# A new tile order for the first convolution of a two-layer attention and long-convolution kernel, with later spectrum stores and earlier exchanges

## The chip, the core and the metric

The kernel runs on one core of a Trainium2 chip. The metric is the device time in microseconds (us), the median of several runs. A profile of one execution gives, beside it, every instruction of the engines: PE (TensorE, matrix products), ACT (ScalarE), DVE (VectorE), POOL (GpSimd) and the DMA queue that SyncE issues (SP). The engines run side by side, each through its own list of instructions in program order, and wait for each other by semaphores. So the *order* in which the program lists its tiles decides which engine waits for which.

## The reference, cut to what matters

Two layers of the same pair are applied to x (2048 positions, 512 channels): a sliding dilated attention `A`, and a long convolution `B` through a Fourier transform.

```python
def _B_ref(u, A_re, A_im, B_re, B_im, C_re, C_im, log_dt, Dskip):
    ...                                            # K: the filter, 512 channels x 2048 taps
    Kp = jnp.pad(K, ((0, 0), (0, L)))
    up = jnp.pad(up, ((0, 0), (0, 0), (0, L)))     # up is u, transposed to channels x positions
    Kf = rfft2(Kp[:, None, :]); Uf = rfft2(up[:, :, None, :])      # abbreviated
    Yf = Uf * Kf[None, :, :, :]
    y = irfft2(Yf, s=(1, L2))[:, :, 0, :L]
    return y.transpose(0, 2, 1) + u * Dskip[None, None, :]

x = x + _A_ref(_layernorm(x), A_wqkv, A_wo)
x = x + _B_ref(_layernorm(x), ...)     # "first convolution": computes Uf and Kf
x = x + _A_ref(_layernorm(x), A_wqkv, A_wo)   # "second front": its layernorm, transposes, K and Q projections
x = x + _B_ref(_layernorm(x), ...)     # the same filter: Kf is read back from memory
```

## The kernel before

The part that matters is the first convolution and what follows it up to the first product of the second attention. The transforms are products on PE in two steps. Work is cut into tiles of 128 x 1024 elements, and each tile goes PE -> two PSUM banks -> a copy ("evacuation") to SBUF by ACT or DVE. A string of tokens fixes the order, and the last letter of a token says who evacuates: `A` is ACT, `D` is DVE.

```python
ORDER0 = """
KA KD KA KD KA KA KD KA KD KA KD kA KD KA KA kD kA kD kA UA KD UA UA UD UA kD UA
UA UD KA UA kD u kD m u u u kA m UA m UD UA u kA m kD u UA u m UA m
UD m UA kA u kD kD u kA u m m kA m u u yD yA m u u m u m yA u yA
yA m m yA m yA yD
"""
ORDERF = """
yA yA yA yA yA yA z00D yA h00 yA z01D h01 z10A z11A h10 a0 p0 h11
n0 z12A z02A a1 z03A h12 S T0 h02 p1 E00A n1 E01A a2 z13A P00 h13 Q00
h03 T1 E10A p2 E11D P01 a3 P02 P03 P10 p3 P11 n2 n3 P12 T2 E20D E21A
P13 T3 E30A P20 P21 x1 P22 P23 E31D
"""
```

There are 16 tokens each of `K` (first step of the filter's transform), `U` (the same of the signal), `k` and `u` (second step), `m` (product of the spectra, on DVE) and `y` (first step back): eight for each of two groups of channels. `z` is the last step (PE, then an addition into x on DVE, or a copy by ACT when PE has added x too). In the second string, `h`, `a`, `p` and `n` are the layernorm's statistics, their sum, its reciprocal root (ACT) and its application (DVE). `T` and `E` are the transposes and their evacuation, `P` and `Q` the projections (four matmuls of 512 columns and one ACT copy), `x` a shifted copy on DVE.

```python
def ptile(self, shape):                     # PSUM tiles: two pools of two, so four in flight
    self.npt += 1
    return self.ps[(self.npt - 1) // 2 % len(self.ps)].tile(shape, F32, name="pb", tag="pb")

def evac(self, dst, src, eng):              # L726
    (self.nc.scalar.copy if eng == "act" else self.nc.vector.tensor_copy)(dst, src)

def k_f2(self, g, ec, eng):
    n = g * NEC + ec
    p2 = self.f2(g, "ka", ec)               # 16 matmuls of 64 columns, L744
    kf = self.nat[n] = self.free.pop(0)     # a slot of SBUF
    self.evac(kf, p2, eng)
    self.nk += 1
    self.pump()
    self.nc.sync.dma_start(self.kf_dram[g, ec]..., kf...)      # L754: store for the second layer

def open_ring(self):                        # called after the last K: eight more slots
    kp2 = self.ring_pool.tile([P, 8, DQG, EC], BF16, name="kf_nat", tag="kp")
    self.free += [kp2[:, i] for i in range(8)]

def pump(self):
    while self.nkf < min(self.nk, self.nm + self.ahead):       # ahead = 4
        self.kf_load(self.nkf); self.nkf += 1

def kf_load(self, n):                       # "exchange": odd and even partitions change places
    kn, ks = self.nat[n], self.free.pop(0)
    for h in range(2):
        sync.dma_start(ks[h::2], kn[1 - h::2])                  # L770
    self.kf[n] = kn, ks

def u_mult(self, g, ec):                    # m: needs ub (from u), kn and its exchanged copy ks
    kn, ks = self.kf.pop(n); ub = self.ub.pop(n)
    for t, k in zip(self.S[g]["t"], (kn, ks)):
        self.nc.vector.tensor_tensor(t[...], ub[:], k, ALU.mult)   # L784
    self.nm += 1
    if self.tag == 0:
        self.free += [kn, ks]
    self.pump()

def u_f2(self, g, ec):                      # u: ub has three buffers; evacuated by ACT, L796
    ...

def i1(self, g, t, eng):                    # y: 16 matmuls of 128 columns, L809/L810
    ...
```

Twelve slots are there from the start. The end of the first attention's layernorm is run beside the first `K` tokens, one closure after each `K` from the second on:

```python
return [lambda: [u_end(8), u_apply(8, range(8, 12), "pool")], lambda: x_stats(14), lambda: x_stats(15),
        lambda: u_begin(12, 16, "dve", "act"), lambda: [u_end(12), u_apply(12, range(12, 16), "pool")]]
```

`u_begin(12, 16, "dve", "act")` sums the statistics on DVE and takes the reciprocal root on ACT, both under one token.

Of the kernel before, what the change touches and what calls it, by code (L numbers as in the profile page):

```python
# [14 lines left out]
F32 = mybir.dt.float32  # L15
# [5 lines left out]
P = 128  # L21
S = 2048
# [15 lines left out]
NG = 2  # L38
DQG = 64
EC = 16  # L40
NEC = 128 // EC
# [6 lines left out]
WUTUxlkKkUkEKkzUzKpzUUqkEzUxpUKxtUUUUUetpqxekQUkkpxKUUkKkpUxEXkkxpUXKXxqpXXqXQgkpKZZZgxx  # L48
"""
ORDER0 = """  # L50
KA KD KA KD KA KA KD KA KD KA KD kA KD KA KA kD kA kD kA UA KD UA UA UD UA kD UA
UA UD KA UA kD u kD m u u u kA m UA m UD UA u kA m kD u UA u m UA m
UD m UA kA u kD kD u kA u m m kA m u u yD yA m u u m u m yA u yA
yA m m yA m yA yD
"""
ORDERF = """
yA yA yA yA yA yA z00D yA h00 yA z01D h01 z10A z11A h10 a0 p0 h11
n0 z12A z02A a1 z03A h12 S T0 h02 p1 E00A n1 E01A a2 z13A P00 h13 Q00
h03 T1 E10A p2 E11D P01 a3 P02 P03 P10 p3 P11 n2 n3 P12 T2 E20D E21A
P13 T3 E30A P20 P21 x1 P22 P23 E31D  # L60
"""
ORDER1 = """
UD UA UA UD UA UA UD UA UD UA UD u UD u m UA u u m UA m u u UA m UD m
# [35 lines left out]
def row_stats(nc, lnst, x_row, a, eng):  # L99
    if eng == "dve":  # L100
        nc.vector.bn_stats(lnst["bn"][:, a, 0, :], x_row)
    else:
        nc.scalar.activation(lnst["junk"][:], x_row, ACT.Identity, accum_out=lnst["s1"][:, a:a + 1])
        row_sumsq(nc, lnst, x_row, a)
# [11 lines left out]
def rstd_act(nc, pool, var):  # L116
    rstd = pool.tile(list(var.shape), F32, name="ln_rstd")
    nc.scalar.activation(rstd[:], var, ACT.Ln, bias=EPS)
    nc.scalar.activation(rstd[:], rstd[:], ACT.Exp, scale=-0.5)
    return rstd  # L120


def ln_begin(nc, pool, lnst, a0, a1, eng, rs="pool"):
    n = a1 - a0
    if eng == "dve":
        ag = pool.tile([P, n, 2], F32, name="ln_ag")
        for a in range(n):
            nc.vector.bn_aggr(ag[:, a, :], lnst["bn"][:, a0 + a, 0, :])
        var, mean, ms = ag[:, :, 1], ag[:, :, 0], -1.0
    else:  # L130
        mean, ms = lnst["s1"][:, a0:a1], -1.0 / D
        msq = pool.tile([P, n], F32, name="ln_msq")
        nc.vector.scalar_tensor_tensor(msq[:], mean, -1.0 / (D * D), mean, ALU.mult, ALU.mult)
        veps = pool.tile([P, n], F32, name="ln_veps")
        nc.vector.scalar_tensor_tensor(veps[:], lnst["s2"][:, a0:a1], 1.0 / D, msq[:], ALU.mult, ALU.add)
        var = veps[:]
    if rs == "act":
        return rstd_act(nc, pool, var), mean, ms
    rstd = pool.tile([P, n], F32, name="ln_rstd")
    nc.vector.tensor_scalar(rstd[:], var, EPS, None, ALU.add)  # L140
    nc.gpsimd.tensor_tensor(rstd[:], rstd[:], lnst["mh"][:, 0:n], ALU.pow)
    return rstd, mean, ms


def ln_end(nc, pool, st):
    rstd, mean, ms = st
    nb = pool.tile(list(rstd.shape), F32, name="ln_nb")
    nc.vector.scalar_tensor_tensor(nb[:], mean, ms, rstd[:], ALU.mult, ALU.mult)
    return rstd, nb
# [6 lines left out]
def ln_apply(nc, out_ap, in_ap, rstd, nb, a, eng):  # L156
    if eng == "act":
        nc.scalar.activation(out_ap, in_ap, ACT.Identity, bias=nb[:, a:a + 1], scale=rstd[:, a:a + 1])  # L158
    else:
        (nc.gpsimd if eng == "pool" else nc.vector).tensor_scalar(out_ap, in_ap, rstd[:, a:a + 1], nb[:, a:a + 1], ALU.mult, ALU.add)  # L160


class LayerA:
# [143 lines left out]
    def core(self, x_sb, u, lnp, ev=None, nprod=0):  # L307

        tc, nc, lnst, l = self.tc, self.nc, self.lnst, self.layer
# [12 lines left out]
        with ExitStack() as c2:  # L322
# [69 lines left out]
            pvs, oTs, lns = {}, {}, {}  # L392
# [20 lines left out]
            def out_proj(a):  # L413
                oT = oTs.pop(a)
                pw = pq_tile()
                xr = x_sb[:, a, :]
                nc.tensor.matmul(pw[:], lhsT=ident[:], rhs=xr, start=True, stop=False)
                for ftp in range(NDT):
                    nc.tensor.matmul(pw[:], lhsT=oT[:, ftp, :], rhs=wo[:, ftp, :], start=False, stop=(ftp == NDT - 1))  # L419
                if a >= 12:  # L420
                    if a >= 14 and l == 1:
                        row_stats(nc, lnst, pw[:], a, "dve")
                    nc.scalar.copy(xr, pw[:])
                else:
                    nc.scalar.activation(xr, pw[:], ACT.Identity, accum_out=lnst["s1"][:, a:a + 1])
                    row_sumsq(nc, lnst, xr, a)

            def x_stats(a):
                row_stats(nc, lnst, x_sb[:, a, :], a, "dve")

            def u_begin(a0, a1, eng, rs="pool"):
                lns[a0] = ln_begin(nc, lnp, lnst, a0, a1, eng, rs)

            def u_end(a0):
                lns[a0] = ln_end(nc, lnp, lns[a0])

            def u_apply(a0, rows, eng=None):
                rstd, nb = lns[a0]
                for a in rows:
                    ln_apply(nc, u[:, :, a, :], x_sb[:, a, :].rearrange("p (q r) -> p q r", r=4), rstd, nb, a - a0,  # L440
                             eng or ("dve" if a % 2 else "act"))
# [47 lines left out]
            for n in range(16):  # L489
# [11 lines left out]
                if n in (8, 12):  # L501
                    u_end(n - 8)
# [12 lines left out]
                if n == 15:  # L515
                    x_stats(13)
                    if l == 1:
                        u_end(8)
                        u_apply(8, range(8, 12), "dve")
# [4 lines left out]
                event(("o", n))  # L524
            if l == 0:
                out_proj(15)
                return [lambda: [u_end(8), u_apply(8, range(8, 12), "pool")], lambda: x_stats(14), lambda: x_stats(15),
                        lambda: u_begin(12, 16, "dve", "act"), lambda: [u_end(12), u_apply(12, range(12, 16), "pool")]]
            u_begin(12, 15, "dve", "act")
            out_proj(15)  # L530
            pw = pq_tile()
# [155 lines left out]
class FftB:  # L687
# [59 lines left out]
    def k_f2(self, g, ec, eng):  # L747
        n = g * NEC + ec
        p2 = self.f2(g, "ka", ec)
        kf = self.nat[n] = self.free.pop(0)  # L750
        self.evac(kf, p2, eng)
        self.nk += 1
        self.pump()
        self.nc.sync.dma_start(self.kf_dram[g, ec].rearrange("p r q e -> (p r) (q e)"), kf.rearrange("p q e -> p (q e)"))  # L754

    def open_ring(self):
        kp2 = self.ring_pool.tile([P, 8, DQG, EC], BF16, name="kf_nat", tag="kp")
        self.free += [kp2[:, i] for i in range(8)]

    def pump(self):  # L760
        while self.nkf < min(self.nk, self.nm + self.ahead):
            self.kf_load(self.nkf)
            self.nkf += 1

# [14 lines left out]
    def u_mult(self, g, ec):  # L779
        n = g * NEC + ec  # L780
        kn, ks = self.kf.pop(n)
        ub = self.ub.pop(n)
        for t, k in zip(self.S[g]["t"], (kn, ks)):
            self.nc.vector.tensor_tensor(t[:, :, ec * EC:(ec + 1) * EC], ub[:], k, ALU.mult)  # L784
        self.nm += 1
        if self.tag == 0:
            self.free += [kn, ks]
        self.pump()

# [457 lines left out]
def kernel(  # L1247
# [16 lines left out]
    nc = tc.nc  # L1264
# [6 lines left out]
    with tc.tile_pool(name="ctmp", bufs=1) as tmp:  # L1271
        consts = build_a_consts(tc, nc, cpool, tmp)
    lnst = dict(s1=cpool.tile([P, NA], F32, name="ln_s1"), s2=cpool.tile([P, NA], F32, name="ln_s2"),
                bn=cpool.tile([P, NA, 2, 6], F32, name="ln_bn"), junk=cpool.tile([P, D], BF16, name="ln_junk"),
                mh=cpool.tile([P, 4], F32, name="ln_mh"))
# [7 lines left out]
    u = xnT[:].rearrange("p t (b r) -> p (t b) r", r=64).rearrange("p q (a r) -> p q a r", r=4)  # L1283
# [5 lines left out]
    lnp = ctx.enter_context(tc.tile_pool(name="ln_small", bufs=3, reuse_waits="tile"))  # L1289
# [5 lines left out]
    kp = kpp.tile([P, P, NA, 4], BF16, name="k_perm", tag="kp")  # L1295
# [26 lines left out]
    with tc.tile_pool(name="ctmp_g2", bufs=1) as g2tmp, tc.manual_schedule(engines=MAN):  # L1322
# [9 lines left out]
        late = la.core(x_sb, u, lnp, ev, 3)  # L1332
# [4 lines left out]
    fb = FftB(tc, nc, C, consts["ident"], w2_dram, g2_dram, kf_dram, x_sb, 0)  # L1337
# [1 line left out]
    fb.ahead = 4  # L1339
    fb.open_mid()  # L1340
    with tc.manual_schedule(engines=MAN):
        fb.run(ORDER0, u, k=kp, late=late)
    fb.c_mid.close()
    la.close()
    la = LayerA(tc, nc, consts, lnst, A_wqkv, A_wo, 1, xnT, 1)
# [1 line left out]
    with tc.manual_schedule(engines=MAN):  # L1347
# [21 lines left out]
        def last(*ops):  # L1369
            def f():  # L1370
                for op, *ix in ops:
# [6 lines left out]
                     e=lambda ft: la.front_ext(3, "dve", ft))  # L1378
        fb.run(ORDERF, None, more=front)
        la.front_close()  # L1380
# [11 lines left out]
    fb = FftB(tc, nc, C, consts["ident"], w2_dram, g2_dram, kf_dram, x_sb, 1)  # L1392
# [48 lines left out]
```

## Time and profile before

| | before |
|---|---|
| device time, median of three runs | 435.77 us (435.69 to 436.33) |
| span of the profiled execution | 434.5 us |
| busy over the span: PE, DVE, ACT | 351.9, 393.2, 322.4 us |
| first matmul of the first convolution | 202.32 us |
| last product `m` of the first convolution | 252.46 us, 0.69 us long |
| first product of the second attention (L295) | 287.98 us |

Times are counted from the start of the span. A row of the groups or of the timeline names the line, the engine, the operation, the tile written, the tiles read, the shapes and the number of instructions. Behind it stand the time and, in brackets, the idle time before it and what ended it. The chain of waits is the path followed back from an end to its causes, and "windows" give each engine's busy time in a stretch. A busy time sums durations that overlap a little, so the step from one instruction's start to the next on the same engine is the better cost of one: eight evacuations that the ACT timeline shows as one run of 7.47 us cost about 0.91 us each.

### The profile page before, as it was taken

To read this page: it belongs to the slowest core of one execution; us is meant where nothing else is said; L and a number is where in the kernel's file an instruction comes from. 1 tells how busy PE (TensorE), PEld (TensorE's weight loads), DVE (VectorE), ACT (ScalarE), POOL (GpSimd) and SP (SyncE) were. 2 spreads that over 40 slices of the span, in tenths; PEclk is the share of its full clock that TensorE was granted. 3 is DMA by queue.
4 is the path that set the end of the run, shared out by engine and by line. 5 is a ranking of instruction groups with operands and counts; after the bars stand their busy time and mean duration, and the time that the engine had idled before them with its cause. 6 is when DMAs were issued, how large, how long until landed. Compare 5 with 4: busy or idle time off the path is not lost.

```text
span 434.5 us, 12684 instructions
## 1 busy us (share of the span) xinstructions
PE 351.9 (81%) x5459; PEld 265.1 (61%) x5502; DVE 393.2 (90%) x549; ACT 322.4 (74%) x544; POOL 54.9 (13%) x46
## 2 busy tenths in 40 slices
PE   3000359998999899999887799999999899997795
PEld 1000117666765568767887798555557787777794
DVE  8999999999999999996889859879999999889874
ACT  6999969676364479987799897864555559689962
POOL 2004040260594000001400000000000020000000
PEclk9999998999999999999899999999999999999999
DMA  8921462122014645572165640860033066225405
GB/s 226 390 86 24 77 68 68 34 60 63 17 44 140 175 142 177 152 317 100 63 255 189 252 124 2 224 213 2 2 94 78 2 232 229 79 97 141 154 27 170
DMA packets 62467, 54.17 MB, mean 125 GB/s; under 512 B 33893, under 2 KB 50890, under 8 KB 61130
## 3 DMA queue, kind: packets, MB, share of 16 engines
q1 hardware_dynamic: 62266, 53.22, 40.0%
q8 instruction: 43, 0.70, 0.7%
q10 hardware_dynamic: 144, 0.13, 0.2%
q14 instruction: 14, 0.11, 0.1%
HBM read 30.28 MB, written 13.24 MB: 100 GB/s over the span
## 4 chain that ended last, share of the span: by engine, by line
PE 41%; DVE 17%; ACT 14%; DMA 5%; SPq 3%; issue 2%; POOL 2%; ACTq 0%; DVEq 0%; POOLq 0%
PE po L407 7%; DVE prod L295 5%; DVE A_t L983 5%; PE pq L348 4%; ACT a1s L726 4%; PE pq L419 4%; PE L L302 3%; PE pb L809 3%; PE pp L242 3%; PE pb L810 2%; ACT ub L796 2%; PE pq L185 2%; DVE pav L399 2%; PE pb L737 2%; PE pk L1135 2%
## 5 line engine op out<-in xcount | busy, mean ns | idle before, releaser
L399 DVE TENSOR_TENSOR pav<-attn,v_ext 128x4096 bf16<-128x4096 bf16 x32 | 72.7, 2282 | 0.7 <-DMA v_ext<-v_ext 0.7
L295 DVE TENSOR_TENSOR prod<-qT,kT_ext 128x4096 bf16<-128x4096 bf16 x29 | 66.3, 2306 | 0.2
L407 PEld LDWEIGHTS <-pav 128*128 128x128 bf16 x1024 | 58.6, 98 | 12.3 <-DVE pav L399 8.7
L407 PE MATMUL po<-ident,pav 128*128 128x128 bf16 x1024 | 62.5, 219 | 3.9 <-DVE pav L399 3.9
L1068 PE MATMUL pt<-ident,x_blk 128*128 128x128 bf16 x64 | 7.2, 261 | 40.0 <-ACT x_blk L158 38.8
L983 DVE TENSOR_TENSOR A_t<-A_t,pow_t 128x1024 bf16<-128x1024 bf16 (+4 forms) x46 | 38.2, 871 | 0.2
L796 ACT CAST ub<-pb 128x1024 bf16<-128x1024 f32 x32 | 32.9, 1086 | 2.7 <-DVE t L784 2.5
L1078 PE MATMUL pp<-xnT,kT_ext 128*128 128x512 bf16 x87 | 25.9, 421 | 10.7 <-ACT xnT L1071 8.3
L350 ACT CAST v_ext<-pq 128x512 bf16<-128x512 f32 x32 | 18.7, 587 | 20.4 <-PE pq L348 16.5
L809 PE MATMUL pb<-Wp,t 128*128 128x128 bf16 x256 | 30.1, 219 | 3.1 <-ACT ub L796 2.7
L744 PE MATMUL pb<-a1s,w_sb 128*128 128x64 bf16 x768 | 27.6, 194 | 5.8 <-ACT ub L796 3.5
L302 PEld LDWEIGHTS <-prod 128*128 128x128 bf16 x928 | 27.0, 96 | 8.5 <-DVE prod L295 3.1
L348 PE MATMUL pq<-wv,xnT 128*128 128x512 bf16 x118 | 30.2, 379 | 1.2 <-ACT v_ext L350 0.7
L1068 PEld LDWEIGHTS <-x_blk 128*128 128x128 bf16 x64 | 5.1, 117 | 42.6 <-ACT x_blk L158 40.9
L726 ACT CAST a1s<-pb 128x1024 bf16<-128x1024 f32 x30 | 29.3, 1074 | 1.8 <-PE pb L737 1.7
L410 ACT CAST oT<-po 128x512 bf16<-128x512 f32 x32 | 18.6, 580 | 15.9 <-PE po L407 15.8
L744 PEld LDWEIGHTS <-w_sb 128*128 128x128 bf16 x768 | 25.1, 98 | 8.3 <-issue 7.1
L810 PE MATMUL pb<-WpJ,t 128*128 128x128 bf16 x256 | 30.1, 219 | 0.0
L419 PE MATMUL pq<-wop,oT 128*128 128x512 bf16 x110 | 29.3, 379 | 0.9
L1059 POOL TENSOR_TENSOR ln_rstd<-ln_rstd,ln_mh 128x4 f32<-128x4 f32 x4 | 20.3, 5080 | 72.3 <-DVE ln_rstd L1054 65.6
L726 DVE CAST a1s<-pb 128x1024 bf16<-128x1024 f32 x18 | 21.7, 1222 | 7.5 <-PE pb L737 7.3
L302 PE MATMUL L<-ind,prod 128*128 128x8 bf16 x928 | 27.5, 166 | 0.7 <-DVE prod L295 0.5
(226 smaller groups left out, 876.3 us busy)
## 6 DMA issues: line engine op xcount, KB each, us to landing
w_sb<-w_dram SPq DMA_DIRECT2D x8, 1024.0 KB, 8.3
w_dram<-w_zero SPq DMA_DIRECT2D x1, 4096.0 KB, 15.1
kf_ring<-kf_dram SPq DMA_DIRECT2D x13, 256.0 KB, 3.8
kf_ring<-kf_dram SPq DMA_DIRECT2D x26, 128.0 KB, 3.7
v_ext<-v_ext SPq DMA_DIRECT2D x4, 784.0 KB, 6.0
x_blk<-in_A_x_dram SPq DMA_DIRECT2D x4, 512.0 KB
kT_ext<-in_A_wqkv_dram SPq DMA_DIRECT2D x4, 512.0 KB, 6.3
x_sb<-in_A_x_dram SPq DMA_DIRECT2D x4, 512.0 KB, 7.9
```

Of the source, the lines that this page charges most:

```text
L295: nc.vector.tensor_tensor(pr, self.qT[q][:, ft].unsqueeze(1).to_broadcast([P, W, 4, P]), kap, ALU.mult)
L302: self.nc.tensor.matmul(L[:, al, w, ft * 8:(ft + 1) * 8], lhsT=pr[:, w, al, :], rhs=self.c["ind8"][:], start=(ft == 0 and w == 0 and al % ...
L348: nc.tensor.matmul(pp[:], lhsT=xnT[:, dt, a * P:(a + 1) * P], rhs=wv[:, dt, :], start=(dt == 0), stop=(dt == NDT - 1))
L399: nc.vector.tensor_tensor(pv[:], attn[:, n % 4].unsqueeze(2).to_broadcast([P, W, DH, H]), vap, ALU.mult)
L407: nc.tensor.matmul(po[:, ft, :], lhsT=pvf[:, w, ft * P:(ft + 1) * P], rhs=ident[:], start=(w == 0 and ft == 0), stop=(w == W - 1), skip_gr ...
L419: nc.tensor.matmul(pw[:], lhsT=oT[:, ftp, :], rhs=wo[:, ftp, :], start=False, stop=(ftp == NDT - 1))
L726: (self.nc.scalar.copy if eng == "act" else self.nc.vector.tensor_copy)(dst, src)
L744: nc.tensor.matmul(p2[:, j, :], lhsT=self.w2[:, ec * EC + j, :], rhs=a1s[:, ec * EC + j, :], start=True, stop=True)
L796: nc.scalar.copy(ub[:], p2)
L809: nc.tensor.matmul(p3[:, j, :], lhsT=t1[:, dql, :], rhs=wp_r, start=True, stop=False)
L810: nc.tensor.matmul(p3[:, j, :], lhsT=t2[:, dql, :], rhs=wpj_r, start=False, stop=True)
L983: return lambda: nc.vector.tensor_tensor(*args)
```

## The change

Four things change, all in the first convolution and in the second front:

1. Both order strings are replaced by newly searched ones; the second convolution's order stays.
2. The store of each filter spectrum to memory is issued when its product `m` has been listed, no longer right behind its evacuation.
3. An exchange is also asked for when enough slots are free for all filter tiles still to come, not only within four of the products.
4. The closure that summed the statistics and took the root is split in two, and the order in which the closures run is a string of its own.

```diff
 ORDER0 = """
-KA KD KA KD KA KA KD KA KD KA KD kA KD KA KA kD kA kD kA UA KD UA UA UD UA kD UA
-UA UD KA UA kD u kD m u u u kA m UA m UD UA u kA m kD u UA u m UA m
-UD m UA kA u kD kD u kA u m m kA m u u yD yA m u u m u m yA u yA
-yA m m yA m yA yD
+KD KA KA KD KA KA KD KA KD KA KD kA kA KD kA KD UA UD UA UD UA kD UA UD UA KD
+kA kD u kD kA u UA m KD m u u UD UA UA UA m UD u m KA UD u m u kA kD m kA UA
+kD u kA m kA kD u m u kA m m u u yD yA u m yA u m m m u u m m
 """
+LATE0 = "a s t g r b"
 ORDERF = """
-yA yA yA yA yA yA z00D yA h00 yA z01D h01 z10A z11A h10 a0 p0 h11
-n0 z12A z02A a1 z03A h12 S T0 h02 p1 E00A n1 E01A a2 z13A P00 h13 Q00
-h03 T1 E10A p2 E11D P01 a3 P02 P03 P10 p3 P11 n2 n3 P12 T2 E20D E21A
-P13 T3 E30A P20 P21 x1 P22 P23 E31D
+yA yA yA yA yA yA yD yA yA yA z01D yD yA yA z00A z10A z11A h01 h00 h10 a0 z12A
+p0 h11 z02A n0 a1 z03A h02 S T0 p1 E01D n1 E00A h12 a2 z13A P02 P01 h03 T1
+E10A Q00 E11D p2 P03 P00 n2 h13 P10 P12 a3 T2 E21D E20A p3 n3 P11 P13 P23 P21
+T3 E31D x1 E30A P20 P22
 """
@@ the closures of the first attention's end
+            def u_aggr(a0, a1): ...            # the sums, DVE
+            def u_rstd(a0): ...                # the root, ACT
-                return [lambda: [u_end(8), u_apply(8, range(8, 12), "pool")], lambda: x_stats(14), lambda: x_stats(15),
-                        lambda: u_begin(12, 16, "dve", "act"), lambda: [u_end(12), u_apply(12, range(12, 16), "pool")]]
+                return {"a": lambda: [u_end(8), u_apply(8, range(8, 12), "pool")], "s": lambda: x_stats(14), "t": lambda: x_stats(15),
+                        "g": lambda: u_aggr(12, 16), "r": lambda: u_rstd(12),
+                        "b": lambda: [u_end(12), u_apply(12, range(12, 16), "pool")]}
@@ k_f2
-        self.nc.sync.dma_start(self.kf_dram[g, ec]..., kf...)
@@ pump
+    def room(self):
+        return self.tag == 0 and len(self.free) > NG * NEC - self.nk
     def pump(self):
-        while self.nkf < min(self.nk, self.nm + self.ahead):
+        while self.nkf < self.nk and (self.nkf < self.nm + self.ahead or self.room()):
@@ u_mult
         if self.tag == 0:
+            self.nc.sync.dma_start(self.kf_dram[g, ec]..., kn...)
             self.free += [kn, ks]
@@ the caller
+        late["."] = lambda: None
-        fb.run(ORDER0, u, k=kp, late=late)
+        fb.run(ORDER0, u, k=kp, late=[late[c] for c in LATE0.split()])
```

## The prediction

> **What bounds the kernel now.** The page's totals come first, and they only say that no engine is idle much. The regime that is changed has to be read by itself, so I cut it into windows with the busy time of each engine (columns: stretch, length, then PE, weight loads, DVE, ACT and POOL, granted clock, DMA share, GB/s).
>
> ```profile
> PE 351.9 (81%) x5459; PEld 265.1 (61%) x5502; DVE 393.2 (90%) x549; ACT 322.4 (74%) x544; POOL 54.9 (13%) x46
> ```
>
> ```profile
> 202.30:208.80 6.50, 4.62 (x147) 4.22 (x147) 4.84 (x11) 4.83 (x8) 3.70 (x5) 1.00 0.33 135
> 208.80:213.40 4.60, 4.60 (x98) 4.25 (x98) 3.55 (x4) 3.26 (x4) 2.35 (x4) 0.63 0.02 4
> ```
>
> ```profile
> 222.00:232.00 10.00, 8.19 (x242) 7.59 (x240) 9.40 (x13) 10.00 (x12) 0.00 (x0) 1.00 0.60 222
> 232.00:242.00 10.00, 8.14 (x237) 7.49 (x233) 9.96 (x15) 10.00 (x12) 0.00 (x0) 1.00 0.50 183
> 242.00:252.00 10.00, 8.04 (x168) 7.73 (x166) 8.46 (x14) 8.58 (x10) 0.35 (x1) 1.00 0.71 257
> 252.00:262.00 10.00, 10.00 (x167) 9.81 (x165) 4.69 (x8) 9.91 (x12) 0.00 (x0) 1.00 0.38 107
> ```
>
> From 222 to 242 both copying engines are full: no order alone shortens that. The slack lies in two places: the first 11 us, and 242 to 252. The instructions of DVE and ACT in time order, each with its wait in brackets, show what the slack is.
>
> ```profile
> 203.45 1.23 DVE L726 CAST a1s<-pb 128x1024 bf16<-128x1024 f32 x1 [3.65 <-PE pb L737]
> ...
> 207.86 0.16 DVE L148 SCALAR_TENSOR_TENSOR ln_nb<-ln_ag,ln_rstd 128x4 f32<-128x4 f32 x1 [0.51 <-ACT ln_rstd L119]
> ...
> 212.56 1.23 DVE L726 CAST a1s<-pb 128x1024 bf16<-128x1024 f32 x1 [0.74 <-PE pb L737]
> ...
> 247.64 2.50 DVE L784 TENSOR_TENSOR t<-ub,kn 128x1024 bf16<-128x1024 bf16 x4 [1.54 <-DMA kn<-w_sb]
> ```
>
> ```profile
> 207.38 0.21 ACT L118 ACTIVATE ln_rstd<-ln_ag 128x4 f32<-128x4 f32 x1 [1.50 <-DVE ln_ag L128]
> ...
> 248.44 1.01 ACT L796 CAST ub<-pb 128x1024 bf16<-128x1024 f32 x1 [1.42 <-DVE t L784]
> ```
>
> The root at 207.38 sits in ACT's list before the next evacuation, and DVE's sum comes late: ACT stands for 1.50 us, PE's PSUM tiles aren't emptied, and PE idles. The wait at 247.64 is an exchange. The chain of waits (start, duration, what) tells why it is late:
>
> ```profile
> 241.33 1.12 ACT kn L726
> 242.44 0.30 SPq L754
> 242.80 0.53 SPq L770
> 243.38 4.17 DMA kn<-w_sb
> 247.64 0.70 DVE t L784
> 248.44 1.02 ACT ub L796
> 249.50 0.22 PE pb L809
> ```
>
> The queue had stores (L754) in front, each held until its own evacuation ended; the exchange (L770) went out at 242.80 and took 4.17 us. DVE waited for it, ACT for DVE through the three `ub` buffers, PE for ACT.
>
> After the last `m` (252.46, so ended at 253.06 at a step of 0.60) PE is the bound: in the last window it is busy 10.00 of 10.00. Eight `y` of the second group can only start then, and PE runs without a hole to the last `y`, whose matmuls end at about 261.2. From there to the first product of the second attention (287.98) PE is nearly full too.
>
> **What the skill says.** Four places bear. (1) Perfetto Trace Analysis, "Optimization Strategy": the bound engine changes between regimes, and one looks for gaps on it inside its own regime. The trace agrees: DVE and ACT until 253, PE after. (2) TensorE: Matmul & The Clock Gate, "What's actually happening": after an idle window of about 3.4 us the array runs at half clock. Here the clock fell to 0.63 over 208.8 to 213.4, right after two waits of PE (0.71 and 1.17 us); a pair of `K` matmuls started every 0.105 us instead of 0.055, so a `K` tile took about 0.85 instead of 0.45. (3) VectorE: DVE Perf Modes, "Why PSUM operands drop a tier": a PSUM source is slower. The trace agrees: DVE copies 128x1024 from PSUM in a step of 1.14 us, and the SBUF copy of L1315 with as many elements takes 0.41 us. So a tile moved from ACT (step 0.905) to DVE costs DVE more than it saves ACT. (4) DMA: Bandwidth & Descriptors, "Two DMAs through the same engine are not ordered": a later use must wait for the completion semaphore. In this stretch stores of 256 KB landed a median of 2.8 to 3.9 us after issue, and a slot can't be written again before.
>
> **The change, part by part.**
>
> *Counts.* From the strings: ACT evacuates 9+8+12+16+14 = 59 tiles before (KA, kA, UA, u, yA over both strings) and 7+10+10+16+13 = 56 after; DVE 21 before and 24 after. DVE also has 16 `m` of two products at 0.60 us. Up to the last `m` DVE has 20 evacuations before and 22 after (9 KD, 6 UD, 6 kD, 1 yD).
>
> *First convolution, DVE.* Before: from 203.45 to 253.06, 49.6 us, with waits of 0.51+0.31+0.74+0.23+0.29+0.52+0.39+0.60+1.54 = 5.1 us in its list. After: 22 x 1.14 = 25.1, 32 x 0.6025 = 19.3, small layernorm work (0.15+2x0.60+0.29+0.1) = 1.75, together 46.1 us. The first token is now a DVE one, so DVE can start when ACT did, at 203.0. If it never waited, the last `m` would end at 249.1.
>
> *Does anything make it wait?* ACT up to the last `u`: 7+10+10+16+2 = 45 tiles x 0.905 = 40.7, plus 0.45 for the root, from about 203.4: it would end at 244.6, well ahead of DVE's last two `m`. PE: 16 `K` at 0.45, 16 `U` at 0.47, 32 `k`/`u` at about 0.53, 3 `y` at 0.90 = 34.4 us, ample, and four tiles ahead at most. I walked the new list by hand with these steps, each tile waiting for the fourth before it to be evacuated: DVE then hardly ever waits, and ACT loses some 2 us near the end, where the `ub` buffers come free with the `m`. The root now comes a `K` after its sum, so ACT's 1.50 us shrink to about 0.1. With PE less idle in the `K` stretch, the half-clock stretch may go too.
>
> *Exchanges.* First group: 12 slots, a spectrum and its exchange take two, so four are exchanged at once, then each `m` frees two. Second group: after the eighth slot block is opened, `room` holds at every `k`, and each exchange goes out right behind its evacuation. By my walk the last is asked for some 36.8 us into the stage and used some 9 us later. The 1.54 us wait on DVE and the 1.42 us on ACT go.
>
> *Stores.* The same sixteen, 4.2 MB, none waiting for a fresh evacuation, so nothing holds the queue. The cost is new: `kn` is put back on the free list with its store just issued. The ninth and tenth `k` take the slots of the third and fourth `m`. By my walk the store of the fourth is issued at about 26 us, lands 3.5 us later at 29.7, and the tenth `k`, on DVE, wants the slot at 29.3. I allow 0.5 us for it, and 0.7 us for small waits that a hand walk doesn't see. Last `m` ends at 249.1 + 1.2 = 250.3: 2.8 us earlier.
>
> *Tail and second front.* Five `y` of the first group now stand behind the last `u`, but they need no late product: PE does them while DVE finishes, and ACT gets about two copied. From the last `m`, PE has 8 `y` x 0.90 and one `z` of 8 matmuls (0.87): 8.1 us, as before (253.1 to 261.2). Then remain seven `z` of 12 matmuls at 1.29 us (before: `z01` of 0.87 and six of 1.29), four `T` at 0.88, fourteen `P`/`Q` at 0.865 up to the one the first product needs: 9.0+3.5+12.1 = 24.6, about 0.4 more of PE than before, since `z00` moves to ACT. Against that, before waits 0.3 and 0.46 us in this stretch, and DVE loses a `z` (1.15) and gains an `E` (0.60). The first `T` waits for `n0`, whose root stands behind the evacuation of `z12` on ACT: some 0.6 us of PE. From last `y` matmul to first product I get 26.5 us against 26.75: 0.3 us gained.
>
> Sum: 2.8 + 0.3 = 3.1 us. Behind 287.98 the program is unchanged and DVE goes on nearly without a hole, so the shift is carried to the end: 435.77 - 3.1 = **432.7 us**.
>
> **The rivals.** *Slot waits take the place of the exchange wait.* For: slots return with a store in flight, and the queue is served in order, so one blocked exchange holds all behind it. Against: sixteen stores at about 0.5 and sixteen exchanges at about 1.15 us of issue are 26 us of a stage of 47. If each of four reuses cost 0.8 us the gain would vanish: about 435.5. *DVE becomes the bound and gives back what ACT gains.* For: DVE has 2 evacuations more (2.3 us) before the last `m`, and must go without waits of the 5.1 us it has now. If half of those stay, the last `m` is at about 252, and the time 434.5. *PE bounds the tail anyway.* True of the 8.1 us and the front, already in the sum; if the front's new `z00` and the wait for `n0` are not made up, 0.7 us of the gain go: 433.4. *The clean case:* no waits at all, 431.5, and with a front that gains 0.5 more, 431.
>
> **Range and chances.** The middle is 432.7. Downwards little is left below 431; upwards the rivals lie at 434.5 to 435.5. I take 430.9 to 435.0 for eight in ten. The stage is some 11% of the span plus the front, and a gain of 2% (8.7 us) would need more than all the waits named; a loss of 2% has no source. Faster 0.02, within 2% 0.97, slower 0.01.
>
> **What would show it.** The `ln_rstd` wait of ACT at about 0.1 instead of 1.50; no DMA in front of an `m`; granted clock near 1 in the first 11 us; DVE waits under 1.5 us up to the last `m`; its end near 250.3, first product near 285; 26.5 us between last `y` and first product. The prediction is wrong if DVE waits for slots (DMA as releaser of an L726 evacuation), if the half-clock stretch comes back longer, or if the front stretches by more than what the convolution gained.

## The result and the profile after

The changed kernel takes 432.75 us (median; 432.67 to 433.83) against 435.73 us for the kernel before in the same set (434.34 to 436.33). The ratio is 0.9942, with a 95% interval of 0.9914 to 0.997: a little faster, inside 2%. In a later set the same kernel gave 432.33 us (431.16 to 434.93), ratio 0.9934 (0.9916 to 0.9952).

The totals have hardly moved; DVE's share is up by two points.

```profile
PE 356.9 (83%) x5506; PEld 266.7 (62%) x5506; DVE 395.2 (92%) x552; ACT 320.3 (74%) x541; POOL 54.9 (13%) x46
```

The windows of the convolution (stretch, length, busy PE, weight loads, DVE, ACT, POOL, granted clock, DMA share, GB/s) show where it went:

```profile
202.30:208.80 6.50, 6.16 (x184) 5.41 (x184) 5.83 (x12) 5.94 (x9) 3.67 (x5) 1.00 0.32 131
208.80:213.40 4.60, 4.60 (x146) 4.22 (x144) 4.44 (x5) 4.60 (x6) 2.36 (x4) 1.00 0.18 60
...
232.00:242.00 10.00, 8.77 (x225) 8.09 (x221) 10.00 (x15) 9.99 (x12) 0.00 (x0) 1.00 0.51 186
242.00:249.00 7.00, 6.43 (x130) 6.02 (x128) 7.00 (x12) 7.00 (x9) 0.00 (x0) 1.00 0.62 226
249.00:257.10 8.10, 7.98 (x136) 7.89 (x137) 3.77 (x5) 6.49 (x8) 0.35 (x1) 1.00 0.97 324
```

Both copying engines are now full to the last `m`, the clock is whole, and then PE is the bound. DVE's and ACT's instructions in time order:

```profile
202.97 1.23 DVE L737 CAST a1s<-pb 128x1024 bf16<-128x1024 f32 x1 [3.21 <-PE pb L748]
...
210.47 4.63 DVE L737 CAST a1s<-pb 128x1024 bf16<-128x1024 f32 x4 [0.16 <-PE pb L748]
...
248.38 0.68 DVE L797 TENSOR_TENSOR t<-ub,w_sb 128x1024 bf16<-128x1024 bf16 x1
...
283.58 2.29 DVE L295 TENSOR_TENSOR prod<-qT,kT_ext 128x4096 bf16<-128x4096 bf16 x1
```

```profile
207.03 0.24 ACT L118 ACTIVATE ln_rstd<-ln_ag 128x4 f32<-128x4 f32 x1
```

Once it has begun, DVE waits 0.16 us in all up to the last `m`, where it had waited 5.13 (waits of 0.15 us or more in the timeline). The root at 207.03 waits for nothing. Four marks cut the span of each profiled execution: first matmul of the stage, end of the last `m` (put 0.60 us, one step, behind its start), first product of the second attention, and first DVE evacuation of the second convolution. The pieces in us, without the 202.3 us ahead of the first mark, which agree within 0.03 us:

| | to last m | last m to first product | first product to second convolution | rest | span |
|---|---|---|---|---|---|
| before | 50.75 | 34.91 | 96.30 | 50.27 | 434.5 |
| changed | 46.69 | 34.60 | 96.96 | 50.36 | 430.9 |
| difference | -4.06 | -0.31 | +0.66 | +0.09 | -3.6 |

At the first product 4.40 us are won; 0.7 are lost again in the second attention, whose program is the same.

### The profile page after: what moved, and what is told of

It is laid out like the page before. It is cut to its first block, busy times and chain, and to the rows that moved or that the text cites. A ratio compares the mean times of both kernels' runs of the same rounds, so it can differ in the third digit from the quotient of the medians.

```text
span 430.9 us, 12739 instructions
## 1 busy us (share of the span) xinstructions
PE 356.9 (83%) x5506; PEld 266.7 (62%) x5506; DVE 395.2 (92%) x552; ACT 320.3 (74%) x541; POOL 54.9 (13%) x46
## 4 chain that ended last, share of the span: by engine, by line
PE 43%; DVE 23%; ACT 7%; DMA 4%; issue 3%; SPq 2%; POOL 2%; DVEq 0%; POOLq 0%; ACTq 0%
PE po L407 8%; DVE A_t L997 5%; PE pq L348 5%; DVE prod L295 4%; PE pq L419 4%; DVE t L797 3%; PE L L302 3%; PE pp L242 3%; PE pq L185 3%; DVE pav L399 3%; PE pb L823 2%; PE pb L824 2%; DVE a1s L737 2%; PE pk L1149 2%; ACT ub L810 2%
## 5 line engine op out<-in xcount | busy, mean ns | idle before, releaser
L407 PEld LDWEIGHTS <-pav 128*128 128x128 bf16 x1024 | 60.1, 99 | 11.4 <-DVE pav L399 7.3
L407 PE MATMUL po<-ident,pav 128*128 128x128 bf16 x1024 | 63.9, 222 | 3.5 <-DVE pav L399 3.5
L1092 PE MATMUL pp<-xnT,kT_ext 128*128 128x512 bf16 x96 | 27.7, 422 | 9.6 <-ACT xnT L1085 8.3
L419 PE MATMUL pq<-wop,oT 128*128 128x512 bf16 x128 | 32.9, 379 | 0.0
L737 DVE CAST a1s<-pb 128x1024 bf16<-128x1024 f32 x22 | 26.1, 1217 | 4.9 <-PE pb L748 4.8
L1073 POOL TENSOR_TENSOR ln_rstd<-ln_rstd,ln_mh 128x4 f32<-128x4 f32 x4 | 20.3, 5080 | 72.2 <-DVE ln_rstd L1068 49.2
L737 ACT CAST a1s<-pb 128x1024 bf16<-128x1024 f32 x26 | 25.6, 1043 | 2.0 <-PE pb L748 2.0
```

Source lines behind the costliest of these rows:

```text
L407: nc.tensor.matmul(po[:, ft, :], lhsT=pvf[:, w, ft * P:(ft + 1) * P], rhs=ident[:], start=(w == 0 and ft == 0), stop=(w == W - 1), skip_gr ...
```

## The experiments

Effects below one per cent drown in the times: 22 runs of one kernel lay between 433.3 and 438.7. So each verdict rests on the marks of the profiled execution, one for each run, with the times beside them. The runs were timed in three sets, and each ratio is against the kernel before in the same set (median 435.38 us for e1, e3, e4 and e7; 435.02 for e2, e8, e9 and e10; 435.35 for e5, e6, e11 and e12). "DVE waits" are those in DVE's list up to the last `m`. Four executions whose convolution met no late exchange (the changed kernel, e8, e9, e11) agree in "to last m" within 0.05 us.

| run | median us, ratio (95%) | to last m | DVE waits, of them for DMA | last m to first product | first product to second convolution |
|---|---|---|---|---|---|
| e1 order and root, old queue | 434.62, 0.9985 (0.9964-1.0006) | 49.27 | 2.41, 2.25 | 34.61 | 96.14 |
| e2 queue changes alone | 433.90, 0.997 (0.995-0.999) | 47.60 | 2.13, 0 | 35.01 | 95.70 |
| e3 root joint | 433.24, 0.9952 (0.9936-0.9969) | 47.32 | 0.67, 0 | 34.58 | 96.96 |
| e4 old front | 433.85, 0.9955 (0.9939-0.9971) | 47.81 | 1.18, 1.02 | 34.84 | 96.97 |
| e5 late stores, old asking | 435.30, 1.0006 (0.9979-1.0033) | 50.60 | 3.61, 3.45 | 36.93 | 95.78 |
| e6 early stores, new asking | 435.20, 1.0003 (0.9975-1.0031) | 49.32 | 2.62, 2.46 | 36.21 | 95.66 |
| e7 old convolution order | 433.06, 0.9942 (0.9921-0.9964) | 46.93 | 1.58, 0 | 34.76 | 96.96 |
| e8 extra matmuls | 432.10, 0.9932 (0.9905-0.9958) | 46.70 | 0.16, 0 | 34.58 | 95.80 |
| e9 z00 on DVE | 433.96, 0.997 (0.9953-0.9986) | 46.74 | 0.16, 0 | 35.48 | 97.06 |
| e10 z00 and n0 first | 434.06, 0.9981 (0.996-1.0003) | 48.09 | 1.47, 1.31 | 35.88 | 98.03 |
| e11 combined | 431.76, 0.9923 (0.9893-0.9953) | 46.69 | 0.16, 0 | 34.45 | 95.94 |
| e12 changed again | 432.33, 0.9934 (0.9916-0.9952) | 47.88 | 1.26, 1.10 | 34.59 | 96.98 |

### Which part pays: order, queue or root

The queue changes taken back (e1):

```diff
-        while self.nkf < self.nk and (self.nkf < self.nm + self.ahead or self.room()):
+        while self.nkf < min(self.nk, self.nm + self.ahead):
@@ store moved from u_mult back to k_f2
```

> The changed kernel with the two queue changes taken back: stores right behind the evacuation, exchanges only within four of the products. Theory (the order pays by taking DVE's waits away; the queue changes only keep exchanges from being late): the waits of the K stretch stay gone, one or two exchange waits of about 1.5 us come back in front of an m, last m near 250.5, time near 434. Rival (the queue changes are what pays): last m at 252 or later, time 435 or more. Second rival (the queue changes do nothing in the new order): 432.7.

The queue changes alone, on the kernel before (e2):

```diff
-        while self.nkf < min(self.nk, self.nm + self.ahead):
+        while self.nkf < self.nk and (self.nkf < self.nm + self.ahead or self.room()):
@@ store moved from k_f2 to u_mult; ORDER0, ORDERF and the closures as before
```

> The kernel before with the two queue changes alone (stores at the product, exchanges when slots are free), old orders and old closures. Theory: the exchange wait of 1.5 us in front of an m goes, the ACT wait with it, unless slot reuse behind a store in flight replaces it; last m near 251.6, time near 434.3. Rival (queue changes are worthless without the order): 435.7. Rival (they pay all): 432.7.

The old convolution order in the changed kernel (e7):

```diff
@@ ORDER0 is the old string; ORDERF the new one without its first five yA (they stand in the old ORDER0)
```

> Old first-convolution order with the new front order; new queue rules and split closures kept. Theory: with early exchanges the 1.5 us DMA wait in front of an m goes, and the split root takes about 1 us of ACT's wait; the rest of the DVE waits stay: last m near 251.5, time near 434.5. Rival (order is nothing, queue and root are all): last m near 249, time 432.7. Rival (queue and root nothing): 435.5.

e7 decides: with the queue rules and the split root, the *old* order reaches 46.93 us to the last `m`, and the new one 46.69. The rival "order is nothing, queue and root are all" holds for the place of the last `m`; by time too e7 and the changed kernel can't be told apart. e1 says the same from the other side: the new order with the old queue stands at 49.27, with three waits for exchanges of 2.25 us together. Its last `m` (251.56) and its time (434.62) lie between what the theory and the first rival expected. And e2, the queue changes alone, goes from 50.75 to 47.60, with its last `m` ended at 249.88, some 1.7 us earlier than its theory had it.

Not all of those 3.15 us are the queue's. e2 has the same instructions as the kernel before up to the first stores, yet DVE's list there is shorter:

```profile
207.82 0.16 DVE L148 SCALAR_TENSOR_TENSOR ln_nb<-ln_ag,ln_rstd 128x4 f32<-128x4 f32 x1 [0.51 <-ACT ln_rstd L119]
207.90 4.61 DVE L726 CAST a1s<-pb 128x1024 bf16<-128x1024 f32 x4
...
223.70 1.88 DVE L786 TENSOR_TENSOR t<-ub,w_sb 128x1024 bf16<-128x1024 bf16 x3
```

From 207.90 four evacuations run without a gap, where the kernel before had waits of 0.31 and 0.74 us for PE. Its first `m` started at 225.26, and this one's at 223.70. The stage began 0.04 us apart, so some 1.5 us came of the half-clock window from 209.0 to 212.4 that the one execution had and the other had not. Without it the kernel before would stand near 49.2, and the queue changes give some 1.6 us: the exchange wait of 1.54. e1 lies no lower than that: without the queue changes, order and root bring nothing. This estimate is a difference of two executions; how often the kernel before meets that window wasn't measured. From e2 (47.60) to e7 (46.93) the split root is added (and the new second front, which comes behind the last `m`): 0.67 us.

The times bear it out. In the set of e12 five executions of the kernel before and six of the changed kernel had a mean granted clock of at least 0.999 over the span, so hardly any half-clock window. They took 433.61 to 434.22 us before and 431.16 to 431.72 changed: 2.65 us between the medians, without an overlap. In the set of e1 the medians of such executions are 434.28 us for the kernel before (eleven) and 434.24 for e1 (five). So half-clock windows are not the source of the gain, and order and root without the queue changes give none.

### The split root

```diff
-LATE0 = "a s t g r b"
+LATE0 = "a s t g b"
+    g0, r0 = late["g"], late["r"]; late["g"] = lambda: [g0(), r0()]
```

> The changed kernel with sum and root under one K token again. Theory: ACT waits for DVE's sum some 0.5 us at the root, PE has tiles in flight and DVE is the bound, so at most 0.3 us: 432.7 to 433.0. Rival (the split root is what emptied the first 11 us of waits): ACT's wait of 1.5 us returns, the clock dip with it, and the time is 434.

Last `m` at 47.32 instead of 46.69: the split is worth 0.63 us, of which 0.51 are DVE's wait for the root, back again. That is more than expected. ACT waits 0.65 us for the sum, not the rival's 1.5, and the clock stayed whole in this stretch.

### Half a queue change is worth nothing

Stores late but exchanges asked for as before (e5), and the reverse (e6):

```diff
@@ e5
-        while self.nkf < self.nk and (self.nkf < self.nm + self.ahead or self.room()):
+        while self.nkf < min(self.nk, self.nm + self.ahead):
@@ e6
@@ store moved from u_mult back to k_f2, the new condition kept
```

> The changed kernel with exchanges asked for only within four of the products, as before; stores stay at the product. In the kernel with both queue changes taken back the last m stood 49.3 us behind the first matmul of the stage, 2.25 us of it waits for exchanges; in the changed kernel 46.7. Theory (what hurts is a store that waits in the in-order queue for a fresh evacuation while exchanges of older data stand behind it): late stores alone cure it, last m at 46.7 to 47.3, no exchange wait above 0.5 us. Rival (the exchanges are simply asked for too late): about 49.

> The changed kernel with the stores right behind the evacuation again; exchanges asked for when slots are free. Theory: with room every exchange of the second group stands in the queue before its own store, so no store holds up an older exchange there; in the first group four are held back. Last m at 46.7 to 47.5. Rival (stores must be late): about 49.

Both theories fell and the rivals hold: 50.60 and 49.32, with times no faster than the kernel before. The idea was that one blocked store holds older exchanges, and either cure lifts that. The DMA queue of the two shows another thing. It issues one transfer after the other, most of them in 0.45 to 0.6 us, three for each filter tile; in the changed kernel it is issuing almost without a pause from 231.7 to 246.9. The last exchange begins at 244.59 in the changed kernel, at 246.84 in e6 and at 249.58 in e5. The one before it, for which DVE has its long wait in both, begins at 242.68, 245.01 and 245.95. From 231.7 on, 12 halves of exchanges stand in front of that one in all three kernels, but 2 stores in the changed kernel and 6 in e6 and e5. Four stores of 0.58 us are 2.3 us, and e6 is 2.33 later. In e5 two long issues in front (2.02 and 1.96 us, against 1.53 and 1.41 in the changed kernel) make up most of the other 1 us, and a half of the exchange itself takes 2.39 us to issue. What makes an issue long isn't shown. The exchange before the last in the queues of the changed kernel and of e5:

```profile
242.68 1.18 SPq L783 DMA_DIRECT2D w_sb<-kn  x2
```

```profile
245.95 2.90 SPq L783 DMA_DIRECT2D kf_sb<-kf_nat  x2
```

DVE in e5, then in e6:

```profile
250.63 0.69 DVE L797 TENSOR_TENSOR t<-ub,kf_sb 128x1024 bf16<-128x1024 bf16 x1 [2.64 <-DMA kf_sb<-kf_nat]
```

```profile
249.71 0.69 DVE L798 TENSOR_TENSOR t<-ub,w_sb 128x1024 bf16<-128x1024 bf16 x1 [2.46 <-DMA w_sb<-kn]
```

The wait costs twice: PE idles with DVE, and the clock falls. The windows of e5 behind it:

```profile
247.70:251.10 3.40, 0.67 (x13) 0.50 (x9) 0.76 (x2) 3.23 (x4) 0.00 (x0) 1.00 0.43 161
251.10:254.50 3.40, 1.75 (x16) 1.58 (x16) 1.52 (x3) 0.00 (x0) 0.34 (x1) 0.51 0.91 327
```

From the last `m` to the last `y` matmul PE then takes 10.45 us (e6: 9.74) instead of 8.12.

### The second front

```diff
@@ e4: ORDERF is "yA yA yA yA yA" and the old string
@@ e9: z00A in ORDERF is z00D
@@ e10: z00D, and "a0 z12A p0 h11 z02A n0 a1" is "a0 p0 z12A n0 h11 z02A a1"
```

> New first-convolution order, second front in the old order (its five missing y put ahead). Theory: the front gives 0.3 us, so 433.0, with the last m still near 249.0. Rival (a large part of the gain is the front's new order): 434 or more.

> The changed kernel with one token of the front changed: z00 is added by DVE instead of copied by ACT, so PE has 8 matmuls instead of 12 for it. Theory (PE bounds the stretch from the last m to the first product, DVE has room there): 0.3 to 0.4 us earlier at the first product, 432.3. Rival (DVE's statistics are the bound of the front, and 1.15 us more on DVE shows): 433 or more.

> As the kernel with z00 on DVE, and the first block's root before the copy of z12 on ACT, its application on DVE before h11. Theory: PE's wait of about 0.45 us in front of the first transposes goes as well: first product 0.7 to 0.8 us earlier than in the changed kernel, 431.9. Rival (h11, put behind, makes the second block's root late, and PE waits there instead): as with z00 alone, 432.3, or more.

e4: from the last `m` 34.84 us with the old front and 34.60 with the new, so the new front gives 0.24. (Its last `m` is late by an exchange, see below, and so its time, 433.85, comes near the rival's.) e9 and e10 both lose: 0.9 and 1.3 us against the changed kernel. DVE of the changed kernel and of e9, the same stretch:

```profile
256.89 1.40 DVE L113 BATCH_NORM_STATS2 ln_bn<-x_sb 128x6 f32<-128x256 bf16 x4
259.65 2.71 DVE L113 BATCH_NORM_STATS2 ln_bn<-x_sb 128x6 f32<-128x256 bf16 x8 [1.36 <-ACT x_sb L845]
```

```profile
258.21 1.23 DVE L843 TENSOR_TENSOR x_sb<-pb,x_sb 128x1024 bf16<-128x1024 f32 x1 [1.20 <-PE pb L840]
259.35 4.01 DVE L113 BATCH_NORM_STATS2 ln_bn<-x_sb 128x6 f32<-128x256 bf16 x12
```

In the changed kernel `h01` fills DVE's gap at 256.89. In e9 `z00` stands before `h01` in DVE's list and must wait for PE, so the gap stays empty and the statistics end later (263.28 instead of 262.29 is the start of the next step). The statistics on DVE, not PE, set the pace at the head of the front. So the time is the rival's, but its reason, 1.15 us more on DVE, is not what costs: e11 below has the same `z00` on DVE *behind* `h01`, where it runs without a wait, and the next step starts at 262.15:

```profile
258.20 1.21 DVE L855 TENSOR_TENSOR x_sb<-pb,x_sb 128x1024 bf16<-128x1024 f32 x1
```

What the second change of e10 costs beside that of e9, 0.4 us, was not taken apart.

### Where the gain goes in the second attention

The clock in the changed kernel's second attention, by windows:

```profile
330.90:334.30 3.40, 2.13 (x42) 1.34 (x40) 3.40 (x3) 1.86 (x5) 0.00 (x0) 1.00 0.00 0
334.30:337.70 3.40, 3.40 (x33) 3.12 (x31) 3.40 (x3) 0.26 (x1) 0.00 (x0) 0.50 0.00 0
```

PE waits 1.25 us for a value product on DVE, and for one window of 3.4 us behind it the clock is at half. Five matmuls that nobody reads fill the wait (e8):

```diff
+                if n == 3 and l == 1:
+                    pw = pq_tile()
+                    self.warm(pw, 5, wo[:, 0, :])
                 pv_sum(rows[n])
```

> The changed kernel with five extra matmuls of 512 columns on PE in the second attention, put in the wait of 1.25 us that PE has for the fourth value product; they write a PSUM tile that nobody reads. In the changed kernel's profile the clock is at half for one window of 3.41 us right there, and the gain of 4.4 us at the first product of the second attention is 3.6 us at the end. Theory (the half-clock window eats 0.8 to 1.2 us): the window goes and the time is 431.6 to 431.9. Rival (the loss is of the program, not of the clock): 432.7 or a little more, since PE gets more to do.

The matmuls of the same sum in the changed kernel, then with the extra ones in e8 (L211):

```profile
334.02 3.38 PE L407 MATMUL po<-ident,pav 128*128 128x128 bf16 x32 [1.25 <-DVE pav L399]
```

```profile
332.95 1.24 PE L211 MATMUL pq<-wop,ident 128*128 128x512 bf16 x5
334.33 1.85 PE L407 MATMUL po<-ident,pav 128*128 128x128 bf16 x30
```

The window is gone, and the piece takes 95.80 us instead of 96.96: 1.16 us. All seven executions with a half-clock window in this piece have 96.96 to 98.03, the others 95.66 to 96.30. The medians (432.10, a little above what was expected, and 432.75 and 432.33 without the extra matmuls) go the same way, but their intervals overlap.

An obvious rival is that the window would have stayed away by chance: the kernel before, e1, e2, e5 and e6 have the same wait (1.24 to 1.25 us) without extra matmuls, and their clock stays whole here. Their traces tell the two cases apart. In every trace with more than one, the half-clock windows start a whole number of 3.413 us apart (kernel before: 65.61, 208.97 and 434.25). Cut on this grid of its own, each trace has a window at this place with the least PE work: 2.02 to 2.15 us in the seven executions that then ran at half clock, 2.53 to 2.69 in the five that didn't, and 3.21 in e8 and 3.12 in e11, which has the extra matmuls too. That of the kernel before:

```profile
335.26:338.68 3.42, 2.53 (x46) 1.65 (x44) 3.42 (x2) 2.58 (x7) 0.00 (x0) 1.00 0.00 0
```

So the loss goes with where the wait falls against this grid, which the change did not aim at, and the extra matmuls raise PE's work above both groups.

### The changed kernel once more, and a combination

> The changed kernel as it is, for the spread and as the base of this set. Theory: last m at 46.7, or up to 1.3 more where an exchange lands late (the last one is issued some 3 us ahead of its use); a half-clock window in the second attention in most executions; median 432.5 to 433.5.

The repeat has its last `m` 1.19 us later; its median, 432.33, is a little under the expected range. Its chain of waits:

```profile
243.78 0.60 SPq L783
244.42 0.58 SPq L800
245.11 0.47 SPq L783
245.62 3.85 DMA w_sb<-kf_sb
249.56 0.70 DVE t L797
```

So the last exchange arrives at the edge of being late. Of six executions with this same convolution (the changed kernel, e4, e8, e9, e10, e12) three wait 1.02 to 1.31 us for it and three don't, with issues that began within 0.6 us of each other. Whether the old order (e7, one execution, no such wait) meets this as often isn't known, so on average its 0.24 us may be gone. e11 holds back the stores of the seventh and later products until that exchange is issued. A slot then goes back on the list before its store is issued; that is safe here only because six slots stand in front of the first such slot, and the last three `k` with their exchanges take just six. e11 adds the extra matmuls, and puts `z00` on DVE *behind* `h01`:

```diff
@@ ORDERF
-... z00A z10A z11A h01 h00 ...
+... h01 z00D z10A z11A h00 ...
+            self.pend = getattr(self, "pend", []) + [(g, ec, kn)]
+            if n < 6:
+                self.flush()             # issues the stores in self.pend
...
+        if self.tag == 0 and self.nkf == NG * NEC:
+            self.flush()
```

> The changed kernel with three additions: the five matmuls in PE's wait of the second attention; h01 before a z00 on DVE; and the stores of the seventh and later products held until the last exchange is issued. Theory: last m at 46.7 with no exchange wait, 26.2 us from last y to first product instead of 26.5, no half-clock window in the second attention (95.8 us from first product to the second convolution instead of 97.0), time 431.3. Rival (the h01 move costs as z00 on DVE did before, or the window moves elsewhere): 432.5 or more.

In e11's queue the last exchange goes out at 243.16 instead of 244.59:

```profile
241.87 1.19 SPq L786 DMA_DIRECT2D w_sb<-kn  x2
243.16 1.18 SPq L786 DMA_DIRECT2D w_sb<-kf_sb  x2
```

No wait for an exchange, 26.33 us from last `y` to first product instead of 26.48, no half-clock window in the second attention. It is the fastest of all by its median, 431.76 us, though not by the 431.3 expected, and its runs lie close (431.55 to 432.81). Against the changed kernel of the same set (432.33) the intervals overlap, so the step beyond it is shown by the marks and not by the times. That the held stores are what removed the wait rests on one execution.

## Why the prediction was right

The time was foretold at 432.7 us and measured at 432.75. The cause that it named holds: DVE's waits in the first 11 us and in front of the late products went, and the last `m` came earlier by them. That the number fits within 0.05 us is luck, since the terms were off in both directions.

- **"If it never waited, the last `m` would end at 249.1."** Measured 248.98. With the 0.16 us that DVE did wait, counting its instructions by their steps was right to 0.3 us.
- **"I allow 0.5 us for it, and 0.7 us for small waits."** Mis-sized, and in the wrong place. The tenth `k` never waited for its slot and there were no small waits. What exists is a wait of 1.0 to 1.3 us for the last exchange, in half of the executions; the profiled one had none, so the convolution gave 4.06 us and not 2.8. In e12 it gave 2.87.
- **"By my walk the last is asked for some 36.8 us into the stage and used some 9 us later."** This failed. Its issue began 42.3 us in (244.59 less 202.29) and its `m` stands 3.8 us behind. The walk let the queue issue when data and slot were ready, and left out the issuing itself, which had been counted elsewhere (26 us of a stage of 47) but lies packed together at the end.
- **"The 1.54 us wait on DVE ... go."** Right, and only by both queue changes at once (e1, e5, e6).
- **What pays.** The prediction put the 5.1 us of DVE's waits down to the order, the root and the exchange together, without a share for each. The runs give the order 0.24 (e7), the root 0.63 (e3), the exchange about 1.6, and the half-clock window of the one profiled execution before about 1.5. The last is not counted for the change: e2, where PE too is busy for only 4.62 of the first 6.50 us, missed the window as well. Whether the change keeps such windows out, with PE now busy for 6.16 of them, isn't shown.
- **"8.1 us, as before"** for the tail: 8.12. **"26.5 us against 26.75"** for the front: 26.48 against 26.74, though the count behind it, PE work, isn't the bound of its first part (e9, e11).
- **"So the shift is carried to the end."** Failed: of 4.40 us at the first product, 3.6 arrive. One half-clock window costs 1.16 (e8), set off in part by a wait of 0.72 us for `v_ext` that the profile before had in this piece and the changed kernel has not.

So a gain put 1.3 us too small and a loss of 0.7 not foreseen partly cancelled: the profiled span fell by 3.6 us and the median by 3.0, where 3.1 was foretold. The rival of the slot waits named the right kind of trouble, a queue that holds up exchanges, though not the right place.

## What to carry to other kernels

An in-order DMA queue has its own budget: add the issue times of everything that stands before the transfer you need, not only when its data are ready. Test a change of several parts by taking each back: here a long searched order was worth 0.24 us to the last `m`, and two small queue rules, useless singly, some 1.6. When one profiled execution has a half-clock window and the other has not, take its cost out before you share the gain among the parts. A wait of PE of some 1.25 us can be worth filling with a few spare matmuls where such a window was seen behind it.

## What the hardware showed beside it

The clock fell to half for a whole window of 3.4 us although PE had been busy for 2.13 of the 3.40 us before. The Trainium skill (TensorE: Matmul & The Clock Gate, "What's actually happening") has half clock follow an idle window of about 3.4 us, and says that these windows run freely. The length and the free running agree (3.413 us and the grid above), but the window need not be idle: 2.02 to 2.15 us of PE work were too little in the second attention. Which execution is hit depends on where its grid lies. Up to 209.0 us the kernel before and e2 have the same work; on its own grid the one has 1.53 us of PE work (205.56 to 208.97) and then ran at half clock, the other 1.69 (205.16 to 208.58) and did not. One limit for all work does not come out of the traces: in the kernel before a window with 1.74 us (246.52 to 249.93), and in e12 one with 1.51 (63.23 to 66.65), were followed by the whole clock.
